# Both passes of a three-stage kernel by seven products for eight, with one class for the layers

## The chip, the cores and the metric

The kernel runs on one core of a Trainium2 chip. PE (TensorE) multiplies matrices, DVE (VectorE), ACT (ScalarE) and POOL (GpSimd) work element by element, and SP (SyncE) issues most of the transfers between the chip's memory and SBUF. The metric is device time in microseconds of one execution.

## What is computed

Four batches of twelve heads of sigmoid attention, 448 positions of 64 numbers each; then two layers on the 1792 tokens, each 768 to 2048 to 768:

```python
scores = scale * np.matmul(q, k.transpose(0, 1, 3, 2)) - np.log(S)
attn = 1.0 / (1.0 + np.exp(-scores))
x = np.matmul(attn, v)            # then to (B * S, H * D)
...
h = x @ w_in                      # first layer
x = (h - np.tanh(h)) @ w_out
...
h = x @ w_in                      # second layer
r = np.maximum(h, 0.0)
return (s * (r * r) + b) @ w_out
```

The layers' weights arrive as 64-bit floats and are turned into 32-bit ones on the chip.

## The kernel before

The tokens are taken in two passes of two batches, 896 tokens each. A pass is an attention over 12 pairs of heads and then the two layers. Line 82 of the profile is the helper that records every instruction in program order, so all rows carry that line and are told apart by the names of their tiles.

*Attention.* For pair `i`, `qk(i, c)` makes a chunk of scores (tile `sc`, then ACT's sigmoid into `af`), `prep(i + 1)` turns the next pair's q and k on PE by the identity (`tqk`) and splits them into high and low parts (`qt`, `kt`, and an unsplit copy `qkf`), and `av(i - 1)` multiplies by the values (`o`). An engine takes its instructions strictly in the order written. Between these steps stand loads, conversions and splits of the first weights, on DVE alone, since ACT is full of sigmoids.

*Precision.* Each product of the layers is three matmuls, high by high, high by low and low by high. A split is a copy on ACT (`whi`, `g`, `x`) and a subtraction on DVE (`wlo` and so on).

*Weights.* A chunk of 128 x 768 numbers is loaded as pairs of 32-bit words (`raw`), converted in four steps (`w_conv`: an ACT or DVE multiply into `wy`, a DVE shift of every second word into `wa`, two DVE steps with two sources into `wa` and `wf`), written to scratch memory and split. In the second pass chunks come from the scratch as `wf`. `w_in` is taken by four chunks to a group, `w_out` by four more, and four groups make a layer.

*First pass.* `layer1`, `layer2`: for each of four chunks of a group `hidden` makes 6 x 3 matmuls on 512 and on 384 tokens (tile `h`), 144 to a group. Then come the output products (`y` 144 matmuls to a group, `z` 168). The order of the work beside them is written by hand: `w_ahead` is called at fixed places and loads, converts or splits the next chunks.

*Second pass.* The class `Second` makes a pair of chunks by two token halves as a two-by-two block product with seven block products for eight (Winograd's form): sums and differences of the four weight blocks (`ws`) and of the four token blocks (`xo`, "t1" to "t4") are split, multiplied in PSUM banks `hs`, and added (`p`). A pair is 7 x 3 x 3 = 63 matmuls of 448 columns. A `Plan` collects all of its operations with an engine, a guessed cost and the keys that they read and write. Then `emit` goes through them as a list scheduler: PE and SP keep their written order, and ACT, DVE and POOL take from what is ready the one that is due first. What it emits is a fixed program; the costs are used for the order only.

*Seam of the passes.* The first scores of the second attention are made between the last `z` products. SBUF is split for good between the attention's tiles, the conversion's and the layers', with a few pools released for the second pass.

Of the kernel before, what the change touches and what calls it, by code (L numbers as in the profile page):

```python
# [19 lines left out]
def tile_kernel(ctx, tc, q, k, v, w_in1, w_out1, w_in2, w_out2, s_in, b_in, out):  # L20
# [16 lines left out]
    nc = tc.nc  # L37
# [26 lines left out]
    at_p = tc.alloc_tile_pool(name="at", bufs=1, side="right")  # L64
    conv_p = tc.alloc_tile_pool(name="conv", bufs=1)
    ps_p = tc.alloc_tile_pool(name="ps", bufs=1, space=PSUM)
    late = {}
# [18 lines left out]
    def banks(name):  # L86
        return ps_p.tile([P, 2, 512], F32, tag="two", name=name, bufs=3)

    turn = [0]

    def bank(name):

        turn[0] += 1
        return banks(name)[:, 0] if turn[0] % 5 % 2 == 0 else ps_p.tile([P, 512], F32, tag="one", name=name, bufs=2)
# [16 lines left out]
    scratch, raw_t, f_t, w_t = {}, {}, {}, {}  # L111

    def w_load(n, alone=False):
        if n >= len(chunks):
            return
        key = chunks[n]
        if key not in scratch:
            t = conv_p.tile([P, WE, 2], U32, tag="raw", name="raw", bufs=3)
            a = CC if key[0] == "in" else 2
            sp.dma_start(out=t.rearrange("p (a f) t -> p a f t", a=a), in_=w_src(key))  # L120
            raw_t[n] = t
        else:
            t = w_p.tile([P, WE], F32, tag="wf", name="wf", bufs=5)
            sp.dma_start(out=t, in_=scratch[key])
            f_t[n] = t

    def w_conv(n, alone=False):

        if n >= len(chunks) or n in f_t:
            return
        key = chunks[n]
        r = raw_t.pop(n)
        a = conv_p.tile([P, WE], U32, tag="wa", name="wa", bufs=2)
        y = conv_p.tile([P, WE], F32, tag="wy", name="wy", bufs=2)  # L140
        t = w_p.tile([P, WE], F32, tag="wf", name="wf", bufs=5)
        if alone:
            dve.tensor_scalar(y, r[:, :, 1].bitcast(F32), 2.0 ** -112, None, op0=ALU.mult)
        else:
            act.activation(y, r[:, :, 1].bitcast(F32), AF.Copy, scale=2.0 ** -112)
        yield
        dve.tensor_scalar(a, r[:, :, 0], 29, None, op0=ALU.logical_shift_right)
        yield
        dve.scalar_tensor_tensor(out=a, in0=y.bitcast(U32), scalar=3, in1=a, op0=ALU.logical_shift_left, op1=ALU.bitwise_or)
        dve.scalar_tensor_tensor(out=t.bitcast(U32), in0=y.bitcast(U32), scalar=0x80000000, in1=a, op0=ALU.bitwise_and, op1=ALU.bitwise_or)  # L150
        scratch[key] = dram.tile([P, WE], F32, name=f"w{key[0]}{key[1]}_{key[2]}_{key[3]}")
        sp.dma_start(out=scratch[key], in_=t)
        f_t[n] = t

    def w_split(n, alone=False):
        if n >= len(chunks):
            return
        t = f_t.pop(n)
        hi = w_p.tile([P, WE], F32R, tag="whi", name="whi", bufs=4)
        lo = w_p.tile([P, WE], F32R, tag="wlo", name="wlo", bufs=4)  # L160
        (dve.tensor_copy if alone else act.copy)(hi, t)
        yield
        dve.tensor_tensor(out=lo, in0=t, in1=hi.bitcast(F32), op=ALU.subtract)
        w_t[n] = (hi, lo)

    done = {w_load: 0, w_conv: 0, w_split: 0}

    def upto(step, n, **kw):

        while done[step] <= (n if step is w_load else min(n, len(a_pass) - 1)):  # L170
            yield from step(done[step], **kw) or ()
            done[step] += 1

    def w_ahead(n, parts="ab"):

        yield from upto(w_load, n + 5)
        for part in parts:
            if part == "a":
                yield from upto(w_conv, n + 3)
            else:  # L180
                yield from upto(w_split, n + 2)

    def now(g):
        for _ in g:
            pass

    def mm3(ps, w, ws, x, xs, first, last):

        pe.matmul(ps, w[0][:, ws], x[:, 0, xs], start=first, stop=False)
        pe.matmul(ps, w[0][:, ws], x[:, 1, xs], start=False, stop=False)  # L190
        pe.matmul(ps, w[1][:, ws], x[:, 0, xs], start=False, stop=last)

    def split(hi, lo, t):
        act.copy(hi, t)
        dve.tensor_tensor(out=lo, in0=t, in1=hi.bitcast(F32), op=ALU.subtract)


    raws, ready, avs, flt, x_t = {}, {}, {}, {}, {}

    def qkv_load(i, what="qkv"):  # L200
        if i >= B * NP:
            return
        b, hs = i // NP, slice(i % NP * 2, i % NP * 2 + 2)
        if "q" in what:
            raws[i] = {"r": at_p.tile([P, 2, D], F32, tag="rawr", name="rawr", bufs=3)}
# [21 lines left out]
    def prep(i):  # L227

        if i >= B * NP:
            return  # L230
        b = i // NP
        rq, rk, rr = (raws[i][nm] for nm in "qkr")
        both = banks("tqk") if i else None


        if i:
            flat = both.rearrange("p a b -> p (a b)")
            parts = [(flat, 0), (flat, SM + P), (flat, SM)]
        else:

            one = [ps_p.tile([P, 512], F32, tag="one", name="tqk0", bufs=2) for _ in range(2)]
            parts = [(one[0], 0), (one[1], P), (one[0], SM), (one[1], 0)]
        for (ps, o), r in zip(parts, (rk, rq) if b % 2 else (rq, rk)):
            for j in range(NJ):
                pe.transpose(ps[:, o + j * P:o + (j + 1) * P], r[:, j].rearrange("p h d -> p (h d)"), ident)
        for ps, o in parts[2:]:
            pe.transpose(ps[:, o:o + P], rr.rearrange("p h d -> p (h d)"), ident)
        tq, tk = (flat[:, 0:S], flat[:, S:2 * S]) if i else (one[0][:, 0:S], one[1][:, RM:P + SM])
        if b % 2:
            tq, tk = tk, tq  # L250
        qt = at_p.tile([P, 2, S], F32R, tag="qt", name="qt", bufs=2)
        kt = at_p.tile([P, 2, S], F32R, tag="kt", name="kt", bufs=2)
        act.copy(qt[:, 0], tq)
        act.copy(kt[:, 0], tk)
        for t, ps in ((qt, tq), (kt, tk)):
            dve.tensor_tensor(out=t[:, 1], in0=ps, in1=t[:, 0].bitcast(F32), op=ALU.subtract)

        flt[i] = tmp_p.tile([P, WN], F32, tag="t2", name="qkf", bufs=2)
        dve.tensor_copy(flt[i], (flat if i else one[0])[:, SM:S + S] if b % 2 else (flat if i else one[0])[:, 0:S + RM])
        ready[i] = qt, kt  # L260
        avs[i] = []

    def qk(i, c):
# [3 lines left out]
        sc = banks("sc")  # L267
# [20 lines left out]
    def av(i):  # L288

        b, hp = i // NP, i % NP  # L290
        rv, af = raws.pop(i)["v"], avs.pop(i)
        o = ps_p.tile([P, 512], F32, tag="one", name="o", bufs=2)[:, :S]

        o2 = ps_p.tile([P, 512], F32, tag="one", name="o2", bufs=2)[:, :SH]
        for c in range(NJ):
            for e in range(2):
                pe.matmul(o[e * D:e * D + D], rv[:, e, c, :], af[c // 2][:, c % 2, e], start=c == 0, stop=False)
        for h in range(2):
            for e in range(2):
                ks = slice(h * RM, h * RM + RM)  # L300
                pe.matmul((o2 if h else o[:, :SH])[e * D:e * D + D], rv[ks, e, NJ, :], af[1][ks, 1, e, :SH], start=h == 1, stop=True)
        yield
        half = tmp_p.tile([P, WN], F32, tag="t1", name="half", bufs=2)[:, :SH]
        act.copy(half, o2)
        dve.tensor_tensor(out=o[:, SH:], in0=o[:, SH:], in1=half, op=ALU.add)
        yield
        if b >= B // 2:
            yield from sums_of_x(b, hp, o)
            return
        if b % 2 == 0:  # L310
            x_t[b // 2, hp] = x_p.tile([P, 2, T2], F32R, tag="x", name="x1", bufs=CC)
        ns = slice(b % 2 * S, b % 2 * S + S)
        xt = x_t[b // 2, hp]
        split(xt[:, 0, ns], xt[:, 1, ns], o)


    def activate(layer, ps, hi, lo, fill):

        n = ps.shape[1]
        t = tmp_p.tile([P, WN], F32, tag="t1", name="t1", bufs=2)[:, :n]  # L320
        g = tmp_p.tile([P, WN], F32, tag="t2", name="t2", bufs=2)[:, :n]
        if layer == 0:
            act.activation(t, ps, AF.Tanh)
            dve.tensor_tensor(out=g, in0=ps, in1=t, op=ALU.subtract)
            next(fill, None)
        else:
# [4 lines left out]
        act.copy(hi, g)  # L331
        next(fill, None)
        dve.tensor_tensor(out=lo, in0=g, in1=hi.bitcast(F32), op=ALU.subtract)
        now(fill)

    pos = [0]

# [750 lines left out]
```

## Time and profile before

| what | us |
|---|---|
| median of 3 runs | 1089.71 (1089.34 to 1090.09) |
| the profiled execution | 1090.19 |
| its span, first to last instruction | 1088.4 |
| PE busy | 1073.2 (99%) |
| DVE busy | 698.7 (64%) |
| ACT busy | 536.5 (49%) |

The span is what the views cover, and the rest of the execution lies around it. Busy shares are means over stages that differ, so they say which engine to look at and not what an edit is worth. TensorE was granted its full clock throughout.

### The profile page before, as it was taken

To read this page: it belongs to the slowest core of one execution; us is meant where nothing else is said; L and a number is where in the kernel's file an instruction comes from. 1 tells how busy PE (TensorE), PEld (TensorE's weight loads), DVE (VectorE), ACT (ScalarE), POOL (GpSimd) and SP (SyncE) were. 2 spreads that over 40 slices of the span, in tenths; PEclk is the share of its full clock that TensorE was granted. 3 is DMA by queue.
4 is the path that set the end of the run, shared out by engine and by line. 5 is a ranking of instruction groups with operands and counts; after the bars stand their busy time and mean duration, and the time that the engine had idled before them with its cause. 6 is when DMAs were issued, how large, how long until landed. Compare 5 with 4: busy or idle time off the path is not lost.

```text
span 1088.4 us, 15221 instructions
## 1 busy us (share of the span) xinstructions
PE 1073.2 (99%) x5933; PEld 933.6 (86%) x5933; DVE 698.7 (64%) x1075; ACT 536.5 (49%) x867; POOL 61.5 (6%) x90
## 2 busy tenths in 40 slices
PE   7999999999999999999999999999999999999998
PEld 4557889888988999999985569999999999999998
DVE  2564656777787657676737778374757982747462
ACT  4775444241536654453527766351515584717170
POOL 4222000000000000000005400000000000000000
PEclk9999999999999999999999999999999999999999
DMA  7574464546445545454454403121112031212002
GB/s 188 153 194 137 131 202 146 174 136 212 131 132 173 191 157 175 144 179 156 140 164 114 105 2 117 44 66 51 58 52 65 15 102 44 73 42 75 30 1 102
DMA packets 104840, 124.47 MB, mean 114 GB/s; under 512 B 50080, under 2 KB 78240, under 8 KB 104768
## 3 DMA queue, kind: packets, MB, share of 16 engines
q1 hardware_dynamic: 100832, 116.94, 35.3%
q0 software_dynamic: 3136, 6.36, 2.1%
q8 instruction: 47, 0.77, 0.3%
q10 hardware_dynamic: 800, 0.20, 0.1%
q14 instruction: 25, 0.20, 0.1%
HBM read 92.80 MB, written 30.67 MB: 113 GB/s over the span
## 4 chain that ended last, share of the span: by engine, by line
PE 95%; DVE 2%; ACT 1%; POOL 1%; issue 0%; ACTq 0%; DVEq 0%; POOLq 0%
PE hs L82 41%; PE h L82 21%; PE z L82 11%; PE y L82 10%; PE o L82 6%; PE sc L82 5%; PE tqk L82 2%; POOL rawv L82 1%; ACT af L82 1%; DVE wa L82 0%; DVE qkf L82 0%; DVE x L82 0%; DVE kt L82 0%; DVE y L82 0%; DVE qt L82 0%
## 5 line engine op out<-in xcount | busy, mean ns | idle before, releaser
L82 PE MATMUL h<-x,whi 128*128 128x512 f32 (+1 forms) x768 | 217.3, 363 | 0.0
L82 PEld LDWEIGHTS h<-x,whi 128*128 128x128 f32 x768 | 141.7, 188 | 17.2 <-issue 0.6
L82 PE MATMUL hs<-xo,whi 128*128 128x448 f32 x504 | 153.4, 368 | 1.3 <-ACT af L82 1.2
L82 PE MATMUL hs<-xo,wlo 128*128 128x448 f32 x504 | 154.2, 368 | 0.0
L82 PE MATMUL h<-x,wlo 128*128 128x384 f32 (+1 forms) x384 | 139.9, 364 | 0.0
L82 ACT CAST whi<-wf 128x768 fp32r<-128x768 f32 x108 | 87.7, 812 | 66.8 <-DVE wf L82 57.1
L82 PE MATMUL hs<-whi,g 128*128 128x384 f32 x448 | 115.2, 335 | 0.0
L82 PE MATMUL z<-whi,g 128*128 128x384 f32 x448 | 115.1, 335 | 0.0
L82 DVE TENSOR_TENSOR wlo<-wf,whi 128x768 fp32r<-128x768 f32 x104 | 99.9, 961 | 19.9 <-ACT whi L82 13.5
L82 DVE TENSOR_TENSOR g<-t,g 128x448 fp32r<-128x448 f32 (+2 forms) x128 | 79.2, 622 | 50.0 <-ACT g L82 49.9
L82 PE MATMUL hs<-g,whi 128*128 128x448 f32 x384 | 110.1, 368 | 0.0
L82 ACT ACTIVATE af<-sc,nlogs 128x896 f32<-128x896 f32 (+1 forms) x96 | 86.2, 927 | 47.6 <-PE sc L82 37.1
L82 PE MATMUL y<-g,whi 128*128 128x384 f32 (+1 forms) x384 | 109.4, 366 | 0.2 <-DVE y L82 0.2
L82 PEld LDWEIGHTS hs<-xo,whi 128*128 128x128 f32 x504 | 94.7, 188 | 11.3 <-ACT af L82 1.5
L82 PEld LDWEIGHTS hs<-xo,wlo 128*128 128x128 f32 x504 | 94.7, 188 | 9.2 <-ACT p L82 0.5
L82 ACT CAST g<-t 128x448 fp32r<-128x448 f32 (+2 forms) x128 | 72.1, 567 | 28.5 <-DVE t L82 26.4
L82 DVE TENSOR_TENSOR y<-hs,y 128x384 f32<-128x384 f32 (+1 forms) x79 | 46.1, 588 | 60.0 <-PE hs L82 59.9
L82 PEld LDWEIGHTS z<-whi,g 128*128 128x128 f32 x448 | 81.0, 188 | 0.6 <-issue 0.6
L82 PEld LDWEIGHTS hs<-whi,g 128*128 128x128 f32 x448 | 81.1, 188 | 0.2
L82 PEld LDWEIGHTS y<-g,whi 128*128 128x128 f32 x384 | 71.2, 188 | 9.1 <-DVE y L82 0.6
L82 PEld LDWEIGHTS h<-x,wlo 128*128 128x128 f32 x384 | 72.0, 188 | 7.6
L82 PEld LDWEIGHTS hs<-g,whi 128*128 128x128 f32 x384 | 72.1, 188 | 7.0
(100 smaller groups left out, 1624.9 us busy)
## 6 DMA issues: line engine op xcount, KB each, us to landing
raw<-in_moe_w_in_dram SPq DMA_DIRECT2D x32, 768.0 KB, 5.2
raw<-in_moe_w_out_dram SPq DMA_DIRECT2D x32, 768.0 KB, 4.7
win<-wf SPq DMA_DIRECT2D x32, 384.0 KB, 2.6
wout<-wf SPq DMA_DIRECT2D x32, 384.0 KB, 2.7
wf<-win SPq DMA_DIRECT2D x32, 384.0 KB, 3.0
wf<-wout SPq DMA_DIRECT2D x32, 384.0 KB, 3.0
rawq<-in_q_dram SPq DMA_DIRECT2D x48, 96.0 KB, 3.5
rawv<-in_v_dram POOLq DMA_DIRECT2D x24, 192.0 KB, 3.6
```

The source lines that it names most:

```text
L82: return lambda *a, **kw: tc.keep_in_program_order(getattr(self.engine, name)(*a, **kw))
```

## The change

- `Second` becomes `Layers(sb)`, used in both passes, and `layer1`, `layer2`, `hidden`, `w_ahead` and the conversion by hand go. So the first pass, too, has seven products for eight and a list that is scheduled, now with conversions in the list. SP is scheduled by due time as well, and a cost can have a busy and a done part.
- A conversion works in place in `raw` (words two apart) and writes `wf`; `wa` and `wy` go. The weight sums are made in place in two `wf` tiles.
- Slots for split weights (`w`), `wf`, `raw` and `p` are taken and given back as their last use is written: 12 `w` slots in the first pass, 18 in the second, where there were 4 + 4 and 14.
- The relu of a stored sum is one DVE step on the sum alone, without ACT's part.
- The identity is built before the value loads are issued.
- The attention's tiles and the layers' share SBUF in turn (`open_pool`, `close_pool`). `prep` of pair 12 is made two tiles ahead of the end of the first pass, and its scores follow in the second attention. Pairs 12 and 13 are loaded in the last output products (`next_loads`), and pair 14 after them.

```diff
-    def w_conv(n, alone=False):
...
-        a = conv_p.tile([P, WE], U32, tag="wa", name="wa", bufs=2)
-        y = conv_p.tile([P, WE], F32, tag="wy", name="wy", bufs=2)
...
-        dve.tensor_scalar(a, r[:, :, 0], 29, None, op0=ALU.logical_shift_right)
...
+        def conv(self, n):
...
+            r, t = self.raw[rk], f_t[k]
+            y, a = r[:, :, 1], r[:, :, 0]
...
+                self.do("ACT", 0.74, lambda: act.activation(y.bitcast(F32), y.bitcast(F32), AF.Copy, scale=2.0 ** -112), w=[("r", rk)])
+            self.do("DVE", 0.47, lambda: dve.tensor_scalar(a, a, 29, None, op0=ALU.logical_shift_right), w=[("r", rk)])
+            self.do("DVE", 0.88, lambda: dve.scalar_tensor_tensor(out=a, in0=y, scalar=3, in1=a, op0=ALU.logical_shift_left, op1=ALU.bitwise_or), w=[("r", rk)])
+            self.do("DVE", 0.88, lambda: dve.scalar_tensor_tensor(out=t.bitcast(U32), in0=y, scalar=0x80000000, in1=a, op0=ALU.bitwise_and, op1=ALU.bitwise_or), r=[("r", rk)], w=[("f", k)])
...
+        def w_pair(self, n):
...
+            self.conv(n)
+            self.conv(n + 1)
...
+            kh, kl = self.w_whole(k0)
...
+            sums = ((v1[:, 1], v1[:, 0], v1[:, 1], ALU.add, k1), (v1[:, 0], v0[:, 0], v1[:, 0], ALU.subtract, k1), (v0[:, 0], v1[:, 1], v0[:, 0], ALU.subtract, k0), (v0[:, 1], v0[:, 1], v0[:, 0], ALU.subtract, k0))
+            for o, a, b, op, k in sums:
+                self.do("DVE", 0.47, lambda o=o, a=a, b=b, op=op: dve.tensor_tensor(out=o, in0=a, in1=b, op=op), r=[("f", k0), ("f", k1)], w=[("f", k)])
...
+            if final and not self.sb:
+                self.next_loads()
+            for t in range(last):
+                if final and not self.sb and t == last - 2:
+                    self.next_prep()
...
+    qkv_load(0, "qk")
+    make_identity(nc, ident)
+    for i, what in ((1, "qk"), (0, "v"), (1, "v"), (2, "qkv")):
...
-    make_identity(nc, ident)
-    prep(0)
+    prep(0, [one("tqk0"), one("tqk0")])
...
+        layers = Layers(sb)
+        layers.early = layers.w_pair(layers.n0)
+        loads = {2: 2, 4: 1, 6: 1, 8: 1, 10: 1}
+        convs = {5: 1, 6: 1, 8: 1, 10: 1}
...
+        layers.run(i1 - 1)
```

POOL at the start of the program, before: the last of nine value loads (`rawv`), which stand behind two loads of `rawr` (the last rows of q and k of pair 0), and then the identity:

```order
L82 DMA rawv<-in_v_dram 64x2x64 x2
L82 DMA rawv<-in_v_dram 128x2x192
L82 DMA rawv<-in_v_dram 64x2x64
masks.py:197 MEMSET ident 128x128
masks.py:199 ISA
masks.py:199 AFFINE_SELECT ident<-ident 128x128
```

and POOL at the same place after the change:

```order
L86 DMA rawr<-in_k_dram 64x2x64
masks.py:197 MEMSET ident 128x128
masks.py:199 ISA
masks.py:199 AFFINE_SELECT ident<-ident 128x128
L86 DMA rawv<-in_v_dram 64x2x64
L86 DMA rawv<-in_v_dram 128x2x192
```

The identity moved ahead of all nine value loads, behind the two loads of `rawr`.

DVE in the first layer of the first pass, in the products by `w_in`, before (`t`, `g`: activation):

```order
L82 TENSOR_SCALAR wa<-raw 128x768
L82 TENSOR_TENSOR g<-t_2626,g 128x512
L82 SCALAR_TENSOR_TENSOR wa<-wy,wa 128x768
L82 SCALAR_TENSOR_TENSOR wf<-wy,wa 128x768
L82 TENSOR_TENSOR t_2662<-h,t_2661 128x384
L82 TENSOR_TENSOR wlo<-wf,whi 128x768
L82 TENSOR_TENSOR g<-t_2662,g 128x384
```

and DVE in the same stretch after the change:

```order
L86 TENSOR_TENSOR wf<-wf 128x3x128 x4
L86 TENSOR_TENSOR y<-hs,y 128x448 x2
L86 TENSOR_SCALAR raw<-raw 128x768
L86 TENSOR_TENSOR w<-wf,w 128x768
L86 SCALAR_TENSOR_TENSOR raw<-raw 128x768
L86 TENSOR_TENSOR p<-hs,p 128x448
L86 TENSOR_TENSOR w<-wf,w 128x768
L86 SCALAR_TENSOR_TENSOR wf<-raw 128x768
L86 TENSOR_TENSOR t<-p,t 128x448
```

The conversion's three steps are now taken apart by other work, and the weight sums (`wf<-wf`) and the sums of kept products (`p<-hs,p`) are new.

PE in the first layer of the first pass, before, a piece of one chunk (numbered `x` tiles are the six input blocks):

```order
L82 MATMUL h<-x_625,whi 128x512 x2
L82 MATMUL h<-x_625,wlo 128x512
L82 MATMUL h<-x_708,whi 128x512 x2
L82 MATMUL h<-x_708,wlo 128x512
L82 MATMUL h<-x_294,whi 128x384 x2
L82 MATMUL h<-x_294,wlo 128x384
```

and PE after the change, from the first group's end on:

```order
L86 MATMUL hs<-g,w 128x448 x132
L86 MATMUL hs<-xo,w 128x448 x108
L86 MATMUL hs<-g,w 128x448 x12
L86 MATMUL hs<-xo,w 128x448 x18
L86 MATMUL hs<-g,w 128x448 x132
```

A group of the first layer has 126 hidden matmuls of 448 columns (108 and 18) where it had 144 of 512 or 384, and the same 144 output matmuls.

## Rows read from the trace of the kernel before

**Rows 1.** The page: engine, busy us (share of the span), instructions

```profile
PE 1073.2 (99%) x5933; PEld 933.6 (86%) x5933; DVE 698.7 (64%) x1075; ACT 536.5 (49%) x867; POOL 61.5 (6%) x90
```

**Rows 2.** Chain of work that ended last: start us, us, what

```profile
89.49 2.94 PE h L82 x12
...
151.28 29.07 PE h L82 x144
...
549.90 0.76 PE tqk L82 x7
...
554.86 0.80 PE sc L82 x5
...
563.11 0.78 PE tqk L82 x7
...
638.40 231.80 PE hs L82 x1130
...
1085.10 0.56 DVE y L82
```

**Rows 3.** Busy us by stage; its columns are in the first line

```profile
core 0: us, PE busy (x) PEld busy (x) DVE busy (x) ACT busy (x) POOL busy (x), PEclk, DMA share, GB/s
...
8.96:89.49 80.53, 77.63 (x618) 44.72 (x618) 42.28 (x72) 57.07 (x92) 21.88 (x35) 1.00 0.69 175
89.49:327.20 237.71, 237.55 (x1173) 209.89 (x1174) 164.35 (x235) 96.81 (x154) 3.01 (x5) 1.00 0.50 157
327.20:563.90 236.70, 236.68 (x1279) 223.07 (x1281) 161.48 (x236) 116.69 (x178) 0.00 (x0) 1.00 0.51 165
...
638.40:871.50 233.10, 233.03 (x1136) 210.33 (x1136) 156.42 (x254) 105.00 (x181) 0.00 (x0) 1.00 0.18 55
871.50:1085.10 213.60, 213.49 (x1140) 204.40 (x1140) 122.20 (x197) 103.11 (x172) 0.00 (x0) 1.00 0.19 59
```

**Rows 4.** PE: longest waits, in us in total, times, longest

```profile
PE tqk L82 <- POOL ident masks.py:199: 4.2, 1, 4.2
```

**Rows 5.** Timeline at the start: start us, us, engine, instruction

```profile
0.74 2.91 SPq L82 DMA_DIRECT2D rawq<-in_q_dram  x4
...
1.99 0.60 POOL L82 DMA_DIRECT2D rawr<-in_k_dram  x1
```

**Rows 6.** DMA issues of the first 20 us: count, KB each, median us to landing

```profile
rawq<-in_q_dram SPq DMA_DIRECT2D x10, 96.0 KB, 3.5
...
rawr<-in_k_dram POOLq DMA_DIRECT2D x1, 32.0 KB, 3.6
```

**Rows 7.** DVE groups by shape: busy us, mean ns of one, idle before

```profile
L82 DVE TENSOR_TENSOR wlo<-wf,whi 128x768 fp32r<-128x768 f32 x104 | 99.9, 961 | 19.9 <-ACT whi L82 13.5 <-PE hs L82 5.2
...
L82 DVE SCALAR_TENSOR_TENSOR wa<-wy,wa 128x768 uint32<-128x768 uint32 x64 | 61.2, 956 | 9.0 <-ACT wy L82 5.2
...
L82 DVE TENSOR_SCALAR wa<-raw 128x768 uint32<-128x768 uint32 x64 | 35.3, 552 | 0.0
L82 DVE TENSOR_TENSOR p<-hs,p 128x448 f32<-128x448 f32 x50 | 30.9, 620 | 17.8 <-PE hs L82 15.1 <-ACT p L82 2.1
...
L82 DVE TENSOR_TENSOR ws<-wf 128x384 f32<-128x384 f32 x32 | 18.6, 583 | 5.5 <-DMA wf<-win 5.4
...
L82 DVE CAST whi<-wf 128x768 fp32r<-128x768 f32 x3 | 1.7, 551 | 0.0
```

**Rows 8.** DVE timeline around one conversion in the first attention

```profile
46.94 0.96 DVE L82 SCALAR_TENSOR_TENSOR wa<-wy,wa 128x768 uint32<-128x768 uint32 x1
47.93 0.96 DVE L82 SCALAR_TENSOR_TENSOR wf<-wy,wa 128x768 uint32<-128x768 uint32 x1
48.81 0.62 DVE L82 TENSOR_TENSOR qt<-tqk,qt 128x448 fp32r<-128x448 f32 x1
49.34 0.61 DVE L82 TENSOR_TENSOR kt<-tqk,kt 128x448 fp32r<-128x448 f32 x1
```

**Rows 9.** PE timeline, two microseconds later

```profile
50.70 1.49 PE L82 MATMUL sc<-qt,kt 64*128 64x448 f32 x12 [0.62 <-ACT half L82]
```

More of the change, by code (lines that the diff above doesn't have):

```diff
@@ L97, in tile_kernel, with __init__, take, give @@
+    class Slots:
+        def __init__(self, n):
+            self.free = list(range(n))
+        def take(self):
+            return self.free.pop(0)
+        def give(self, k):
+            assert k not in self.free
+            self.free.append(k)
     words = [w.bitcast(U32).rearrange("r (c t) -> r c t", t=2) for w in (w_in1, w_out1, w_in2, w_out2)]
@@ L174, in w_ahead @@
[L174 to L198, printed above, removed]
+    scratch = {}
+    W_EARLY, W_LATE, W_MORE, F_SLOTS, R_SLOTS, P_SLOTS = 5, 7, 6, 4, 3, 6
+    w_t = [w_p.tile([P, WE], F32R, tag=f"w{k}", name="w") for k in range(W_EARLY)]
+    f_t = [w_p.tile([P, WE], F32, tag=f"f{k}", name="wf") for k in range(F_SLOTS)]
+    raws, ready, avs, flt = {}, {}, {}, {}
     def qkv_load(i, what="qkv"):
@@ L306, in av @@
         yield
[L307 to L326, printed above, removed]
-            act.activation(t, ps, AF.Relu)
-            dve.scalar_tensor_tensor(out=t, in0=ps, scalar=0.0, in1=t, op0=ALU.max, op1=ALU.mult)
-            next(fill, None)
-            act.activation(g, t, AF.Identity, bias=b_sb, scale=s_sb)
[L331 to L334, printed above, removed]
@@ L845, in group @@
-            a0, c0, vs0 = a, c, vs
+            if first:
+                self.first_pair(n, i)
+            else:
+                now(self.w_pair(n))
+                left = self.pair_open(layer, n, 0, range(NJ - 1) if grp == 0 else None)
+            now(self.w_pair(n + 2))
             m = n + 2
-            a, b = self.bank(), self.bank()
+            a, b = self.b.take(), self.b.take()
             self.prod(a, m, "11", "11", start=True)
@@ new lines, in next_prep @@
+        def next_prep(self):
+            b0, b1 = self.b.take(), self.b.take()
+            self.keys = {"tq": ("b", b0), "tk": ("b", b1)}
+            as_key = lambda ks: [self.keys.get(k, k) for k in ks]
+            prep(2 * NP, [self.whole[b0], self.whole[b1]], lambda eng, cost, fn, r=(), w=(): self.do(eng, cost, fn, as_key(r), as_key(w)))
+            self.b.give(b0)
+            self.b.give(b1)
+    raw_pool = open_pool("raw_w")
+    at = open_pool("qk", side="right")
+    open_pool("raw_qkv", side="right")
```

959 lines of the change are left out of this document (422 added, 537 removed).

## The prediction, made before the changed kernel ran

> **What bounds the kernel now.** I read the page's busy shares first, to see which engine can set the time at all, then the chain that ended last, to see where its links run, then the stages. PE is busy 1073.2 us of a span of 1088.4, DVE 698.7 [rows 1]. The chain shows why that is more than an average: in both passes it is one matmul after another, in pieces of tens or hundreds of us, so a matmul taken out of the stream shortens the time, and anything added on another engine costs nothing until PE has to wait for it [rows 2]. The stages show the room that is left: in the first pass DVE works 164.35 of 237.71 us and then 161.48 of 236.70, ACT 96.81 and 116.69; in the second pass DVE has 156.42 of 233.10 and 122.20 of 213.60 [rows 3]. PE idles for hardly 0.2 us in each of these. Outside them one wait of PE stands out: 4.2 us at the start, for the identity that POOL makes [rows 4].
>
> **The products.** The first pass runs from 89.49 to the end of the transpose at 563.11 + 0.78 = 563.89, which is 474.40 us. In it stand matmuls of the second attention that PE must do in either kernel: 0.76, two of 0.80 (the two score chunks), 0.78, together 3.14 [rows 2]. So the first pass itself is 471.26. Its last pair of heads' value products lie inside, as they do in the second pass. The second pass, which already makes seven products of eight and has 448 columns in each of its first-layer matmuls, runs from 638.40 to 1085.10, or 446.70, with PE never idle [rows 2, 3]. The changed first pass issues the same products in the same shapes, instruction for instruction, so I take the second pass's length for it: **-24.6 us**. A cross-check from the other side: 144 hidden products take 29.07 us now [rows 2]; an eighth of the eight such groups is 29.1. The second pass keeps less than that, since its narrower matmuls take 231.80/1130 = 0.2051 us each against 29.07/144 = 0.2019 for 512 and 384 columns together. I use the smaller gain, since it is measured whole.
>
> **The start.** POOL now builds the identity behind two small loads instead of behind nine more of the values. Then data ends PE's wait. SP's four rawq issues take 2.91 us from 0.74, so the second one starts near 1.5, and a load lands 3.5 us after its issue: about 5.0, or 5.7 if that counts from the issue's end. POOL's last rawr issue is at 1.99 for 0.60, and lands 3.6 later, at 5.6 to 6.2, for the last two of eight transposes [rows 5, 6]. PE's wait ended at 8.96; I take 5.3: **-3.7 us**, between -2.8 and -4.2 (the whole wait [rows 4]). The value loads start later by the identity's few instructions; their first reader stands in the second iteration.
>
> **DVE in the first pass.** Here the change pays. Each pair of input chunks now needs four sums of 384 elements and difference splits of 768, 768, 768 and 384, where it needed two splits of 768; and each pair of hidden chunks needs three additions of kept products. The order counts 379 DVE instructions between the first product of the pass and the last product of the second layer's first pair, the stretch with the densest DVE work (it holds the preparation of the second layer's input): 113 with two sources and 768 elements, 35 shifts, 184 of 448, 45 of 384, 2 small ones of about 0.4. With 0.958, 0.552, 0.620 and 0.583 us each they sum to 108.3 + 19.3 + 114.1 + 26.2 + 0.8 = 268.7 us [rows 7]. That is the upper bound, each instruction behind the end of the last. The lower: qt starts 0.88 us after wf, which lasts 0.96, and kt 0.53 after qt's start, which lasts 0.62; where an instruction is ready it starts some 0.08 before the one ahead ends. wf itself, which reads what wa wrote, started 0.99 after wa of 0.96 [rows 8]. With 0.08 off all 379 the sum is 238.4. PE needs 1185 matmuls there, ten of which the trace counts double, 1195 x 0.2051 = 245.1 us. So PE waits between 0 and 23.6 us. The in-place steps of a conversion read each other's output, while the list puts other work between many of them, so I take the middle, 253.5: **+8 us**, spread over the first layer and the start of the second. Over the rest of the pass DVE has slack: in the whole pass some 634 instructions sum to 453 us, less 51, middle 427, against 446.7. ACT stays far below: 391 instructions for 327, at the present mean of (96.81 + 116.69)/332 = 0.64 us, are some 250 us [rows 3].
>
> The Trainium skill, VectorE: DVE Perf Modes, section The DRAIN you can't avoid, says the opposite of the 0.08: the next Vector instruction does not start until the pipe is empty. By that the upper sum would hold and the wait be 23.6; the trace disagrees wherever the next instruction is ready [rows 8].
>
> In-place conversion removes the wa and wy buffers and no instruction; I cost it at nothing, since a shift reading every second word takes 0.552 us and a cast of contiguous words 0.551 [rows 7]. That no row shows a strided write is the slower rival below.
>
> **Attention and seams.** In the first attention 100 DVE instructions stand for 75, among them a fourth conversion (0.55 + 0.55 + 0.96 + 0.96 = 3.0 us) and the sums of x. One conversion ahead of qt and kt left PE a gap of 0.62 us [rows 9]. In iterations 8 to 10 DVE has two conversions, two odd pairs' sums (seven instructions, some 4.1) and one set of weight sums (2.9): about 25 us with prep's share, 22 after overlap, against three iterations of 80.53/12 = 6.7 [rows 3]. That is 2 to 5 over, of which the next iteration, without prep, takes some back: +2.5. The loads of pair 14 now stand on SP behind the 14 stores of the first pass; pairs 12 and 13 are loaded before them. Their landing of 3.5 us is hidden by pair 12 and 13's scores up to a small rest: +0.5. Together **+3 us**, between 0 and +8. What hides the other new work (POOL's sums, SP's waits for slots, the shared SBUF) is PE's own stream of 446.7; uncovered, each would show as a PE wait in the same place.
>
> **Sum**, on the profiled execution's 1090.19 (span 1088.4 and 1.8 around it): 1090.19 - 24.6 - 3.7 + 8 + 3 = 1072.9. The median of the runs shown is 1089.71, 0.48 lower, so I forecast **1072.4 us**.
>
> **Rivals.** *DVE hidden throughout.* The list starts DVE's work early enough, as it does in the second pass, where PE never waits for it [rows 3]; against it, 238.4 of 245.1 us is a full engine. Then 1090.19 - 24.6 - 3.7 - 0.48 = 1061.4.
>
> *DVE becomes the bound of the first layer.* Each in-order wait on ACT or on the scratch write of a chunk, which the in-place sums must let finish, eats the 0.08. For it speaks that 379 instructions leave no idle time; against it, that DVE ran 164 us in this layer's stage without making PE wait [rows 3]. Price: 23.6 instead of 8, and 6 for attention: 1091.0, no gain at all.
>
> *Slower: words two apart.* After the change, the 120 two-source steps of 60 conversions in the pass read both sources at every second word, half of them write so too. If an operand at that step costs a second element time, each takes longer by twice 0.956 - 0.552 = 0.81 us [rows 7], 97 us in all; DVE then needs 427 + 97 = 524, PE follows it, and the time is 1090.19 + 524 - 471.3 - 3.7 + 3 - 0.5 = about 1142. It decides from 0.37 us an instruction on, where DVE needs 472. Against it stands the shift's 0.552, which is a read only.
>
> The Trainium skill, Vector Engine (DVE) Microarchitecture Reference, section Measured stream behaviour on trn2, has the rule for it: a port runs at full rate only over runs of two adjacent words or more. By its rule the shift ought to be slow too, and the trace disagrees for the read; for a write no run here shows it.
>
> **How the numbers follow.** The likeliest case, with waits of DVE between 3 and 15 us, gives 1066 to 1080 and has 0.55. DVE hidden has 0.19, DVE as the bound 0.15 (1084 to 1093, about half of it faster), words two apart 0.08, a load or a slot that holds up the pass 0.03. A difference under 0.2% (2.2 us) is what a measurement here can't tell from none: faster 0.82, the same 0.06, slower 0.12. The range 1062 to 1088 leaves out the strided case, the upper half of the bound case and a sliver below.
>
> **What would show it.** Right: the first pass's chain in PE pieces of hs, its length 446 to 462 us; PE's first transpose at 5 to 6 us; DVE busy about 420 us in the pass; PE waits there for DVE, most of them around the second layer's first products. Wrong: two-source steps of raw longer than 0.96 us; PE waiting all along the second layer as well; a wait for rawq at the seam; a gap of PE after the last score of the first attention of several us.

## The result and the profile after

The changed kernel takes 1080.57 us (median of 4 runs, 1079.39 to 1081.91) beside 1089.69 for the kernel before on the same chip: a ratio of 0.9917, with a 95% interval of 0.9899 to 0.9934. It is faster by 9.1 us, where 17.3 were forecast; the time lies inside the range, though just outside the 1066 to 1080 that the prediction gave its likeliest case. The profiled execution took 1081.91, its span 1080.1. The page, which answers to [rows 1]:

```profile
PE 1055.4 (98%) x5790; PEld 920.7 (85%) x5790; DVE 793.5 (73%) x1264; ACT 562.8 (52%) x912; POOL 73.2 (7%) x100
```

PE is busy for 17.8 us less and DVE for 94.8 more. The stages, with the columns of [rows 3]: start, first attention, first pass in two parts, second attention, second pass in two parts, end.

```profile
0.00:5.63 5.63, 3.36 (x4) 1.20 (x5) 0.44 (x2) 1.49 (x2) 4.50 (x13) 1.00 0.56 128
5.63:91.66 86.03, 78.91 (x618) 44.48 (x618) 57.83 (x94) 58.46 (x94) 33.34 (x43) 1.00 0.68 176
91.66:318.00 226.34, 223.22 (x1085) 202.00 (x1086) 214.39 (x333) 129.06 (x207) 0.00 (x0) 0.99 0.53 168
318.00:545.31 227.31, 225.93 (x1203) 215.25 (x1201) 195.69 (x306) 119.23 (x187) 7.66 (x12) 1.00 0.50 156
545.31:626.58 81.27, 76.60 (x610) 42.99 (x609) 45.10 (x78) 58.06 (x93) 27.71 (x34) 0.96 0.41 105
626.58:861.00 234.42, 232.91 (x1135) 210.25 (x1136) 159.97 (x262) 108.58 (x185) 0.00 (x0) 1.00 0.20 61
861.00:1076.80 215.80, 214.51 (x1143) 204.49 (x1141) 119.48 (x192) 87.89 (x147) 0.00 (x0) 1.00 0.18 56
```

The differences, stage by stage, before and after. The first pass ends exactly at 545.24, with the first score of pair 12; 0.79 us of transposes for that pair lie inside it and are counted with the second attention, as in the forecast.

| stage | before | after | difference | forecast |
|---|---|---|---|---|
| start | 8.96 | 5.63 | -3.33 | -3.7 |
| first attention | 80.53 | 86.03 | +5.50 | +2.5 |
| first pass | 471.26 | 452.79 | -18.47 | -16.6 |
| second attention | 77.65 | 82.13 | +4.48 | +0.5 |
| second pass | 446.70 | 450.22 | +3.52 | 0 |
| sum | | | -8.30 | -17.3 |

The chain of work, which answers to [rows 2], runs through DVE at the first pass's opening and again around the second layer's start, from 267 to 346 us; for the rest of the pass it is PE:

```profile
96.42 0.97 DVE raw L86
...
112.83 1.08 ACT t L86 x2
115.03 148.51 PE hs L86 x716
267.36 1.06 DVE y L86 x2
...
346.48 198.83 PE hs L86 x1070
```

From 267.36 to 346.48 DVE is busy 78.53 of 79.12 us, so it has no slack left there, but PE waits only 1.29 us of that.

So the products' gain came, and a little more; the two attentions and the second pass gave 13.5 us back. Where PE waited, in us in total, times, longest:

```profile
PE hs L86 <- ACT p L86: 6.6, 7, 2.7
PE sc L86 <- DVE qt L86: 5.4, 2, 2.8
...
PE tqk L86 <- DMA rawq<-in_q_dram: 0.9, 1, 0.9
...
PE hs L86 <- DVE w L86: 0.4, 1, 0.4
```

Three of these waits by PE's timeline, in the first attention, at the first pass's opening and at the second layer's start:

```profile
78.63 1.61 PE L86 MATMUL sc<-qt,kt 64*128 64x448 f32 x10 [2.51 <-DVE qt L86]
...
115.03 5.17 PE L86 MATMUL hs<-xo,w 128*128 128x448 f32 x17 [2.69 <-ACT p L86]
...
330.12 10.14 PE L86 MATMUL hs<-xo,w 128*128 128x448 f32 x48 [1.03 <-ACT p L86]
```

The 4.2 us for the identity [rows 4] are gone and 0.9 for data have come. The DVE groups of a conversion, which answer to [rows 7]:

```profile
L86 DVE SCALAR_TENSOR_TENSOR raw<-raw 128x768 uint32<-128x768 uint32 x64 | 61.2, 956 | 5.0 <-ACT raw L86 2.3 <-DVE raw L86 0.5
L86 DVE SCALAR_TENSOR_TENSOR wf<-raw 128x768 uint32<-128x768 uint32 x64 | 60.8, 954 | 0.9
...
L86 DVE TENSOR_SCALAR raw<-raw 128x768 uint32<-128x768 uint32 x64 | 37.3, 583 | 0.0
```

Reading and writing every second word costs the two-source steps nothing (956 ns before). The shift's mean rose from 552 to 583, and that is not the stride either. In the first attention POOL's sum of x and a shift, by POOL's and DVE's timelines:

```profile
42.56 1.38 POOL L86 TENSOR_TENSOR y<-xo 128x448 f32<-128x448 f32 x1 [1.16 <-DVE xo L86]
```

```profile
42.86 1.50 DVE L86 TENSOR_SCALAR raw<-raw 128x768 uint32<-128x768 uint32 x1
```

The shift starts 0.30 us after POOL and ends 0.42 after it: it lasts 1.50 instead of 0.55, as if it had stood still until POOL was through. The Trainium skill, SBUF — State Buffer, section Who interferes with whom, has this as a rule: DVE and GpSimd share a port pair, a tensor_scalar can be one of the DVE forms that take it, and the engine that comes second is blocked for the whole of the other's instruction. The trace agrees.

In the second attention, DVE around the step with the half split and the four sums, then PE, then the granted clock (in the column before the last two):

```profile
599.27 0.62 DVE L86 TENSOR_TENSOR qt<-tqk,qt 128x448 fp32r<-128x448 f32 x1 [2.03 <-ACT kt L86]
...
606.39 0.62 DVE L86 TENSOR_TENSOR xo<-y,xo 128x448 fp32r<-128x448 f32 x1
606.93 0.54 DVE L86 CAST w<-wf 128x384 fp32r<-128x384 f32 x1
607.51 0.56 DVE L86 TENSOR_TENSOR w<-wf,w 128x384 fp32r<-128x384 f32 x1
608.11 2.34 DVE L86 TENSOR_TENSOR wf<-wf 128x384 f32<-128x384 f32 x4
610.36 0.62 DVE L86 TENSOR_TENSOR qt<-tqk,qt 128x448 fp32r<-128x448 f32 x1
```

```profile
611.04 2.39 PE L86 MATMUL sc<-qt,kt 64*128 64x448 f32 x10 [2.85 <-DVE qt L86]
613.36 0.90 PE L86 MATMUL tqk<-ident,rawk 128*128 128x128 f32 x3
```

```profile
607.00:609.00 2.00, 1.18 (x8) 0.50 (x8) 1.90 (x5) 1.78 (x3) 0.00 (x0) 1.00 0.00 0
609.00:611.00 2.00, 0.00 (x0) 0.00 (x0) 1.93 (x5) 0.00 (x0) 0.00 (x0) 0.69 0.00 0
611.00:613.00 2.00, 1.96 (x10) 1.46 (x10) 1.97 (x4) 0.00 (x0) 0.00 (x0) 0.50 0.00 0
613.00:615.00 2.00, 2.00 (x11) 1.35 (x7) 0.70 (x2) 1.89 (x3) 0.00 (x0) 0.50 0.00 0
```

Behind an even pair of heads, which has two sums and splits of x, DVE is idle for 2.03 us ahead of qt. Behind this odd one, which has seven, they end at 606.93, 3.4 us of weight steps follow, and only then comes qt. PE stands for 2.85 us, and its clock falls to half (1.2 GHz) and stays there for some 6 us: three transposes take 0.90 us, where they take 0.55 at the full clock. PE's busy time in this attention, from its first score, is 76.67 us, and 73.92 in the run after_even below, where the stall is gone and the products are the same: so the stall costs some 2.7 us beyond its length, by the clock.

### The profile page after: what moved, and what is told of

It is laid out like the page before. It is cut to its first block, busy times and chain, and to the rows that moved or that the text cites. A ratio compares the mean times of both kernels' runs of the same rounds, so it can differ in the third digit from the quotient of the medians.

```text
span 1080.1 us, 15112 instructions
## 1 busy us (share of the span) xinstructions
PE 1055.4 (98%) x5790; PEld 920.7 (85%) x5790; DVE 793.5 (73%) x1264; ACT 562.8 (52%) x912; POOL 73.2 (7%) x100
## 4 chain that ended last, share of the span: by engine, by line
PE 80%; DVE 15%; ACT 3%; issue 2%; DMA 0%; DVEq 0%; SPq 0%; ACTq 0%
PE hs L86 70%; PE o L86 5%; PE sc L86 4%; DVE wf L86 3%; DVE xo L86 2%; DVE w L86 2%; PE tqk L86 2%; DVE p L86 2%; DVE raw L86 2%; DVE y L86 1%; DVE t L86 1%; DVE g L86 1%; ACT af L86 0%; ACT w L86 0%; ACT t L86 0%
## 5 line engine op out<-in xcount | busy, mean ns | idle before, releaser
L86 PE MATMUL hs<-xo,w 128*128 128x448 f32 x2016 | 423.7, 369 | 8.4 <-ACT p L86 6.6
L86 PEld LDWEIGHTS hs<-xo,w 128*128 128x128 f32 x2016 | 378.4, 189 | 48.7 <-ACT p L86 10.8
L86 PE MATMUL hs<-g,w 128*128 128x448 f32 x1152 | 239.0, 367 | 0.0
L86 ACT CAST w<-wf 128x768 fp32r<-128x768 f32 (+1 forms) x186 | 145.0, 784 | 180.0 <-PE hs L86 118.4
L86 PE MATMUL hs<-w,g 128*128 128x384 f32 x1344 | 236.9, 336 | 0.0
L86 PEld LDWEIGHTS hs<-w,g 128*128 128x128 f32 x1344 | 234.4, 188 | 0.6
L86 PEld LDWEIGHTS hs<-g,w 128*128 128x128 f32 x1152 | 216.4, 188 | 20.0
L86 DVE TENSOR_TENSOR w<-wf,w 128x768 fp32r<-128x768 f32 (+1 forms) x192 | 170.5, 894 | 67.8 <-ACT w L86 59.1
L86 DVE TENSOR_TENSOR g<-t,g 128x448 fp32r<-128x448 f32 x128 | 77.4, 618 | 16.4 <-ACT g L86 16.4
L86 ACT CAST g<-t 128x448 fp32r<-128x448 f32 x128 | 71.7, 566 | 27.8 <-DVE t L86 26.0
```

The source lines that it names most:

```text
L86: return lambda *a, **kw: tc.keep_in_program_order(getattr(self.engine, name)(*a, **kw))
```

## The experiments

Times are medians; the kernel before stood at 1090.0 to 1090.2 beside them, and ratios are against it. Unless it says otherwise, a run is the changed kernel (1080.57, ratio 0.9917) with the edit shown. The first pass is counted with its 0.79 us of transposes here: 453.58 for the changed kernel, and 81.34 for its second attention.

**behind_prep and earlier** ask whether the place of the weight steps on DVE costs the attentions their time.

```diff
+            if i + 1 < i1:
+                prep(i + 1)
             for _ in range(convs.get(i - i0, 0)):
...
             if i - i0 in (7, 9, 11):
                 next(layers.early, None)
-            if i + 1 < i1:
-                prep(i + 1)
```

> Only the place of the early weight work in the attention loop changes: conversions and splits of the first weights now stand on DVE behind the next pair's qt, kt and qkf, not ahead of them. Theory A (order): PE's gaps in the attentions (sc waiting for DVE qt or qkf: 2.5 and 2.9 us the two longest) come from weight work standing in front, and the half clock after the gap in the second attention from the gap. Then attention 1 goes from 86.0 to 82 to 83 us and attention 2 from 82.1 to 77.5 to 79, in all 5 to 8 us less than the changed kernel. Rival B (amount): DVE simply has too much to do in iterations 8 to 11; the gap moves to the value products, whose bank comes free later, and the total changes by -1 to +2 us.

Measured: 1087.82, ratio 0.9977 (0.9968 to 0.9987), 7 us slower. The first attention took 92.84, the second 81.84. Theory A in this form fell: the order that was to help hurts, and worse than rival B said. PE in the first attention:

```profile
81.02 1.79 PE L86 MATMUL sc<-qt,kt 64*128 64x448 f32 x12 [2.32 <-DVE qkf L86]
...
96.58 0.41 PE L86 MATMUL o<-af,rawv 64*64 64x224 f32 x2 [2.40 <-DVE xo L86]
```

Behind prep the weight steps hold up the value products' bank (`xo` reads it), and the x steps then run into the next prep. The waits named qkf are for PSUM in all likelihood: `sc` and `tqk` share three tiles, and qkf is the last reader of one.

For `earlier`:

```diff
-        loads = {2: 2, 4: 1, 6: 1, 8: 1, 10: 1}
-        convs = {5: 1, 6: 1, 8: 1, 10: 1}
+        loads = {1: 2, 3: 1, 4: 1, 5: 1, 6: 1}
+        convs = {3: 1, 4: 1, 5: 1, 6: 1}
...
-            if i - i0 in (7, 9, 11):
+            if i - i0 in (7, 8, 9, 11):
```

and a `yield` between the second and the third of the four sums.

> Same work and same place ahead of prep, but spread: conversions in iterations 3, 4, 5, 6 for 5, 6, 8, 10, loads earlier to match, and the step with the half split and four sums cut in two (iterations 8 and 9). Theory A (order) and rival B (amount) both give attention 1 some 3 to 4 us back, since two conversions leave the full iterations 8 and 10. In attention 2, which converts nothing, they differ: A gives 3 to 4.5 us back, because no burst ahead of qt is longer than 2.2 us and the clock stays up; B gives under 1.5, because iterations 8 to 11 hold the same work.

Measured: 1078.89, ratio 0.9895 (0.9883 to 0.9908). The second attention fell by 3.0, at the lower edge of A, outside B; but a gap of 2.13 us is left there, and the clock fell behind it, which A had ruled out. The first rose to 88.15, against both: each conversion that is moved to an early iteration brings a gap of its own (1.56, 0.54, 0.82, 0.89 us).

**true_costs** gives the list the durations that the trace shows, in 25 of its lines with a cost on ACT or DVE.

```diff
-            self.do("DVE", 0.54, lambda: dve.tensor_tensor(out=self.pt[o], ...
+            self.do("DVE", 0.62, lambda: dve.tensor_tensor(out=self.pt[o], ...
```

> The costs that the list scheduler is given are set to the durations of the trace (DVE 0.54 to 0.62, 0.88 to 0.96, 0.47 to 0.55 to 0.58; ACT 0.43 to 0.53, 0.74 to 0.84 or 0.92, and so on); nothing else. Theory C: PE's waits in the two passes (hs for ACT p, 6.6 us in 7 waits; hs for DVE, about 1.7) come from a list that believes DVE and ACT some 12% faster than they are and starts weight work too late. Then the first pass goes from 452.9 to 447 to 450 us and the second from 450.2 to 447 to 448.5: 4 to 8 us less. Rival D: the waits come from the first pair of each pass, where everything is due at once and no order helps; then the change is within 1.5 us.

Measured: 1085.16, ratio 0.9957 (0.9945 to 0.9969). C is right for the second pass, 447.94 for 450.22, and wrong for the first, 459.64 for 453.58; D fits neither pass. In the first pass new waits stand at the second layer's start, on PE:

```profile
325.35 1.11 PE L86 MATMUL hs<-xo,w 128*128 128x448 f32 x2 [1.26 <-DVE xo L86]
...
331.24 2.61 PE L86 MATMUL hs<-xo,w 128*128 128x448 f32 x6 [1.50 <-DVE xo L86]
```

The costs of before were not guessed too low: behind a step of 0.62 the next one, if ready, starts 0.53 later, as kt behind qt in [rows 8], so 0.54 is what it costs an engine that is never idle. Here DVE is just that, from 317 to 343 us. In the second pass it is far from it, which may be why the longer costs help there; that was not tried by itself.

**identity_late** undoes the move of the identity.

```diff
-    make_identity(nc, ident)
     for i, what in ((1, "qk"), (0, "v"), (1, "v"), (2, "qkv")):
         qkv_load(i, what)
+    make_identity(nc, ident)
```

> One edit undone: the identity is built behind the nine value loads again. If the start's gain is the identity's and nothing else's, the first transpose is back near 8.96 us from 5.63 and the time is 3.3 us longer than the changed kernel (3 to 3.6). Rival: the first scores wait for something else soon after (loads of pair 1, DVE's zeroing), and part of the 3.3 is taken back: 1 to 2 us.

Measured: 1085.82, 5.2 us longer, ratio 0.9956 (0.9944 to 0.9968). That is longer than either expectation. In the traces, the first transpose came at 8.97, which is the 3.3. The first attention took 87.99, 1.96 longer with the same gaps: here the clock fell to half after its gap of 2.52 us, which it did not do in the changed kernel's own trace. The first pass took 452.10, 1.48 shorter: there the changed kernel's clock fell and this one's did not. So the identity is worth 3.3. The clock makes two traces differ by as much as the rest, but that it makes the difference between the medians is not shown.

**sums_on_act** takes POOL's sum of x away from the conversions.

```diff
-            pool.tensor_tensor(out=f, in0=xo[nm][j][:, 0].bitcast(F32), in1=xo[nm][j][:, 1].bitcast(F32), op=ALU.add)
+            act.copy(f, o)
```

> The copy of x that the attention keeps (y) is made by ACT from the PSUM bank, not by POOL as a sum of the two halves; POOL keeps only the four subtractions of y. In the changed kernel's trace the shift of a conversion takes 1.47 us, not 0.55, when POOL's sum (1.38 us) runs beside it, and ends 0.43 after it. Theory E (DVE waits while POOL reads): in attention 1 both slow shifts go back to 0.55 to 0.6, the PE gaps at iterations 5 and 6 (1.53 and 0.55) fall to about 0.6 and 0, and attention 1 is 1.3 to 2.5 us shorter; attention 2, which converts nothing, keeps its gap of 2.9. Rival F: ACT, full of sigmoids, passes its six further copies of 0.53 us a pass on to the scores, and the time grows by 1 to 3 us.

Measured: 1085.31, ratio 0.9961 (0.9948 to 0.9973). Theory E holds for its mechanism: the shifts of the first attention are back at 0.55,

```profile
L86 DVE TENSOR_SCALAR raw<-raw 128x768 uint32<-128x768 uint32 x4 | 2.2, 555 | 0.0
```

and the gap of 1.53 us at iteration 5 is gone. That at iteration 6 is not: it is 0.80 for 0.55. Rival F holds for the time: ACT's copy waits 0.69 us for DVE and then lasts 0.53, and PE waits 0.7 to 1.1 in every second iteration instead (attentions 87.02 and 83.97, where E had the first shorter by 1.3 to 2.5).

**after_even** moves the early steps of the second attention from behind odd pairs to behind even ones.

```diff
-            if i - i0 in (7, 9, 11):
+            if i - i0 in ((6, 8, 10) if sb else (7, 9, 11)):
```

> In the second attention only, the three early steps on the first weights move from iterations 7, 9, 11 to 6, 8, 10, that is from behind the long sums of an odd pair of heads to behind the short ones of an even pair; same work, nothing split. Theory A (order, as the run that spread the work left it): PE's gap of 2.85 us before qt falls below 1 us and the half clock after it goes, so attention 2 is 3.5 to 4.5 us shorter than 81.3 and the total 3.5 to 4.5 less than the changed kernel. Rival B (amount): a gap of 2 us or more appears at iteration 8 or 10 instead, and the total is within 1 us.

Measured: 1075.94, ratio 0.9874 (0.9861 to 0.9888), 4.6 us less than the changed kernel. The second attention took 76.79 for 81.34, at a clock of 1.00 throughout, with these gaps left on PE:

```profile
601.33 1.49 PE L86 MATMUL sc<-qt,kt 64*128 64x448 f32 x12 [1.55 <-DVE qkf L86]
...
608.63 1.50 PE L86 MATMUL sc<-qt,kt 64*128 64x448 f32 x12 [0.78 <-DVE qkf L86]
```

That is theory A's saving, just above its range, though the gap that is left is 1.55 and not below 1. Of the 4.55, 2.75 are PE's busy time, which is the clock, and 1.8 its waits. The work is the same, so B is out for this attention, and the loss there was the place of these steps.

**second_shift and no_sign_step** load and unload DVE in the first pass.

```diff
+            if not alone:
+                self.do("DVE", 0.47, lambda: dve.tensor_scalar(a, a, 0, None, op0=ALU.logical_shift_right), w=[("r", rk)])
```

> Each of the 60 conversions of the first pass that stand in the list gets one more DVE step, a shift by nothing (0.55 us each, 0.47 from start to start, 28 us in all, 15 of them before the second layer's first pair). Theory G (DVE is nearly full there and any step costs): the first pass is 10 to 28 us longer than 453.6. Rival H (DVE has slack, and the pass's 6 us of loss come only from the first pairs of the two layers): 0 to 5 us longer.

Measured: 1090.14, ratio 1.0001 (0.9992 to 1.0010); the first pass took 461.77, 8.2 more, between G and H.

```diff
-            self.do("DVE", 0.88, lambda: dve.scalar_tensor_tensor(out=t.bitcast(U32), in0=y, scalar=0x80000000, in1=a, op0=ALU.bitwise_and, op1=ALU.bitwise_or), r=[("r", rk)], w=[("f", k)])
```

(with the step ahead of it writing `t`; the steps of the attention keep theirs)

> The last step of the 60 listed conversions (which puts the sign back; the weights of the first pass lose their signs) is left out: 60 x 0.96 us of DVE less, 0.88 from start to start, 53 us in all. Theory G (DVE's load costs the first pass its 6 us over the second): the pass falls to 447 to 449 us, with PE's waits for ACT p and DVE w there gone. Rival H (the waits come from the order at the pass's opening, before most conversions): they stay, and the pass is within 1.5 us of 453.6.

Measured: 1076.41, ratio 0.9874 (0.9860 to 0.9887); the first pass took 447.98, in G's range, though 1.10 and 0.38 us of the waits for ACT p are left, of 4.42 in all. Without its 0.79 of transposes that is 447.2, the 446.7 of the second pass of before within 0.5. So DVE's load is what the first pass loses by, 5.6 us of it, but softly: 28 us more cost 8.2. The list plans anew in both runs, so that they change the order along with the load; what order alone gives is in late_start below.

**first_too** is after_even with the first attention changed alike.

```diff
-            if i - i0 in ((6, 8, 10) if sb else (7, 9, 11)):
+            if i - i0 in ((6, 8, 10) if sb else (7, 11)):
```

> The run after_even, and in the first attention too the step with the half split and the four sums leaves iteration 9: it goes to 11, where no later pair is prepared, and the split that stood there is left to the pass's list. Theory A (order): the gap of 2.51 us before qt in attention 1 goes, and with it the half clock that followed it in most traces (some 2 us); attention 1 falls from 86.0 to 82 to 83.5, while the pass takes the split, 1.4 us of DVE, for under 1 us: in all 2 to 4 us less than 1075.9. Rival B (amount): iteration 10, with a conversion, now shows the gap, or the pass's opening waits longer for its second weights; the total is within 1 us of 1075.9.

Measured: 1077.31, ratio 0.9882 (0.9868 to 0.9897). Theory A is out, and rival B's mechanism holds, though the total is 1.4 above and not within 1: against after_even the first attention fell by 1.7 to 84.33, and the first pass rose by 3.1 to 455.23, with 1.80 us for DVE w at its opening where there were 0.22, and the clock at half behind the next wait there (2.69), which it was not behind the same wait in after_even (2.72). A gap of 0.77 is left at iteration 9.

**pieces** cuts the first attention's steps to at most 1.8 us ahead of qt (`conv` made a generator with a `yield` after each DVE step), and lets DVE make the copy of x there.

```diff
-        convs = {5: 1, 6: 1, 8: 1, 10: 1}
+        loads = {2: 2, 4: 1, 6: 1, 8: 1, 10: 1} if sb else {1: 2, 3: 1, 6: 1, 8: 1, 9: 1}
+        convs = {3: (0, 0), 4: (0, 1), 5: (0, 1), 6: (1, 2), 7: (1, 2), 8: (2, 2)}
...
-            if i - i0 in ((6, 8, 10) if sb else (7, 9, 11)):
+            if i - i0 in ((6, 8, 10) if sb else (10, 11)):
...
+                dve.tensor_copy(f, o)
```

> In the first attention, the DVE steps on the first weights are cut so that at most 1.8 us stand ahead of qt, never behind an odd pair's long sums: three conversions (not four) in pieces over iterations 3 to 8, the first split at 10, the half split and sums at 11. The kept copy of x is made by DVE from PSUM there, not by POOL. The second attention as in the run after_even. Theory A with E (DVE's two idle microseconds ahead of qt are free, and a POOL sum beside it takes one of them): no PE gap above 0.8 us in attention 1, which falls to 79.5 to 82 us; the pass's opening, with a conversion and a split more, loses 1 to 2: 1071 to 1074 in all. Rival B (amount): the work only moves to the pass's opening, whose waits of 3 us double, and the total is 1075 or more.

Measured: 1074.27, ratio 0.9856 (0.9839 to 0.9872). The first attention fell to 81.21, as theory A with E had it, though with a gap of 1.03 (0.8 was its limit). The first pass took 454.02, 1.9 more than in after_even, and the total is 0.3 above theory A's range and 0.7 below B's. What B said of the pass's opening is seen there, in one wait of 4.39 us where there were 0.44 and 2.69; DVE, ACT and PE there:

```profile
92.17 0.96 DVE L86 TENSOR_TENSOR w<-wf,w 128x768 fp32r<-128x768 f32 x1
93.04 0.56 DVE L86 TENSOR_SCALAR raw<-raw 128x768 uint32<-128x768 uint32 x1
...
97.22 0.96 DVE L86 SCALAR_TENSOR_TENSOR wf<-raw 128x768 uint32<-128x768 uint32 x1
98.10 0.39 DVE L86 TENSOR_TENSOR hs<-hs,half 128x224 f32<-128x224 f32 x1
```

```profile
99.19 0.53 ACT L86 CAST xo<-hs 128x448 fp32r<-128x448 f32 x1 [4.36 <-DVE y L86]
...
100.35 0.54 ACT L86 COPY p<-hs 128x448 f32<-128x448 f32 x1
```

```profile
100.94 3.63 PE L86 MATMUL hs<-xo,w 128*128 128x448 f32 x10 [4.39 <-ACT p L86]
```

The list put a split and two conversions, 5.9 us, ahead of the sum of the last values. It takes DVE as free when the pass begins (87.05); DVE comes from the attention's last x steps at 92.05. ACT's `p` copy stands behind a cast that waits for that sum, and PE behind `p`.

**late_start** is pieces with DVE's and ACT's true start told to the list, and the costs of true_costs for the second pass alone.

```diff
-            free = dict.fromkeys(waiting, 0.0)
+            free = {**dict.fromkeys(waiting, 0.0), **late}
...
-            self.plan.emit()
+            self.plan.emit({} if self.sb else {"DVE": 5.0, "ACT": 4.4})
```

> On top of the run pieces, two edits of the list only, one for each pass, read apart by stage. First pass: the list is told that DVE is free 5.0 us and ACT 4.4 us after the pass begins (as that run's trace has it), where it took all engines as free at once; the order then has the last values' sum ahead of two conversions on DVE. Second pass: costs as long as the durations of the trace, as in the run true_costs, where this pass took 447.9. Theory I (PE's wait of 4.39 us at the pass's opening is that wrong start): the wait falls under 1.5 us and the first pass from 454.0 to 449 to 451.5; with 448 for the second, 1067.5 to 1070.5 in all. Rival J (DVE has too much to do at the opening, whatever the order): the wait moves to the next pair's weights, the first pass stays within 1 us of 454.0, and the total is 1071.5 to 1073.

Measured: 1066.45, ratio 0.9781 (0.9767 to 0.9794). DVE and the stages (first attention, first pass, second attention, second pass):

```profile
92.66 0.39 DVE L86 TENSOR_TENSOR hs<-hs,half 128x224 f32<-128x224 f32 x1
92.96 0.55 DVE L86 TENSOR_SCALAR raw<-raw 128x768 uint32<-128x768 uint32 x1
```

```profile
5.43:86.67 81.24, 77.44 (x617) 44.63 (x618) 53.70 (x92) 59.35 (x95) 25.99 (x37) 1.00 0.65 172
86.67:538.01 451.34, 447.91 (x2285) 415.76 (x2286) 412.16 (x644) 248.43 (x394) 7.68 (x12) 1.00 0.53 165
538.01:614.62 76.61, 73.72 (x610) 41.82 (x609) 45.18 (x78) 56.96 (x92) 27.75 (x34) 1.00 0.46 117
614.62:1062.30 447.68, 446.48 (x2278) 414.99 (x2276) 281.31 (x454) 197.24 (x333) 0.00 (x0) 1.00 0.19 58
```

Theory I: PE's wait of 4.39 at the opening is gone, with one of 1.43 us at 108 us and one of 1.31 late in the pass; the first pass took 451.34, 2.7 less, and the second the expected 448; the total is 1 us below its range. This version takes 14.1 us less than the changed kernel and 23.6 less than the one before: the first attention gave 4.8, the first pass 2.2, the second attention 4.7, the second pass 2.5.

## Why the prediction was right and wrong

*The products, right.* -24.6 was the second pass's length put for the first's. With DVE unloaded the first pass comes to 447.2, which is -24.1.

*DVE in the first pass, near in size, wrong in place.* The +8 measured +6.1 (452.79 less 446.70), and no_sign_step shows that 5.6 of it go with DVE's load. It was to lie around the second layer's first products; there it was 1.29 us (1.03 and 0.26). Most lay at the opening: 0.44 for DVE w and 2.69 for ACT p, and behind the latter the clock was at half for some 3 us (PE's busy time in the pass is 449.07, and 447.81 in after_even's trace, where it did not fall: 1.3). DVE was busy 410 us of the forecast 420, and around the second layer's start, where the text had it full, it was (78.53 of 79.12 us). But PE waited only 1.29 us there and more at the opening, so that 6.1 lies near 8 is in part luck.

One reading in that term needs setting right. The prediction says that the Trainium skill, VectorE: DVE Perf Modes, section The DRAIN you can't avoid, is against the 0.08. The same section adds that a next op which is not held starts earlier, so starts 0.88 and 0.53 us apart [rows 8] do not contradict it.

*The start, right.* -3.33 for -3.7, with PE waiting for data as said; the loads landed 0.3 later than taken.

*Attention and seams: here the prediction failed.* Its step "+3 us, between 0 and +8" measured +9.98. For the first attention it added up DVE's work over three iterations and let the next take the surplus back: +2.5, measured +5.50, of which pieces gives 4.8 back. What counts is the place: two microseconds ahead of qt are free behind an even pair and none behind an odd one (after_even, pieces), and PE's gap shows as soon as they are exceeded. It also counted POOL's sums among the work that PE's stream hides; in the first attention two shifts beside them took 0.95 us longer each, on the path to qt. For the second attention it priced only the loads of pair 14, at +0.5, and these cost nothing that shows: no PE wait there names a load. The weight steps, at new places there too, were left out: measured +4.48, of which after_even gives 4.55 back.

*The second pass: a term that was missing.* The text took its length for both passes and did not cost the second one's own new order. It lost 3.52: 2.6 in four waits for ACT's `p` copies, the rest in PE's busy time (447.42 for 446.52 in [rows 3]). Longer costs in the list take 2.3 to 2.5 back (true_costs, late_start), so it is the order; which of the moved steps does it was not tried. That the time stayed in the range all the same is the range's width: two terms priced at +3 and 0 measured +9.98 and +3.52.

*The rivals.* DVE hidden throughout is out by 6.1 us. DVE as the bound, at 23.6, is out by 17.5 the other way: the chain does run through DVE for 79 us, but PE waited 1.29 us there and not at all between 346 us and the pass's end. Words two apart is out by [rows 7] beside the rows above, 956 and 954 ns.

*Where the gain went.* Of 17.3 us, 8.3 came, 9.0 did not: 7.0 in the attentions and 3.5 in the second pass, plus 0.4 at the start, less 1.9 that the first pass did better. The run late_start changes only orders, the costs and starts that the list goes by, and the engine that makes one copy, and it gets 14.1 back.

## What to carry to other kernels

Price a burst on an in-order engine by the slack at its own place (what is due right behind it, and what was just ahead), not by the work of a few iterations. A list scheduler's plan is as good as its first state: tell it when each engine really comes free, and give it costs from start to start for an engine that is full. When the bound falls in one stage, cost the other stages' new orders as well, since a few stalls of 0.4 to 3 us, and the slower clock behind some of them, took back 13.5 of a gain of 25.

## What the hardware showed that was not expected

TensorE's granted clock fell to half (1.2 GHz) behind some of PE's stalls and stayed there for 3 to 7 us (10 in true_costs, behind several), and the same stall did it in one execution and not in the next. Seven traces have the 2.5 us at iteration 9 of the first attention, and it fell in five of them; behind the 2.7 to 2.9 us of the second attention it fell in six of six. In second_shift it fell behind waits of 1.31, 1.40 and 0.87 us close together, and in true_costs behind those from 321 to 331 us. In late_start, whose longest wait after the start is 1.57, it did not fall after the start. So a stall can cost twice its length. The runs of one kernel lie up to 2.5 us apart (1079.39 to 1081.91); that this is the reason is not shown, since one execution of each was traced.

At the start the column of the granted clock does not tell PE's speed. In five of the twelve traces since the change it shows half from 8 to 12 us, where PE waits twice for about 1 us; in the other seven, and in that of the kernel before, it shows 1.00. Yet in just those eight the first three transposes take 0.87 to 0.90 us, as at half the clock, and in the five 0.52; late_start and after_even:

```profile
5.43 0.87 PE L86 MATMUL tqk<-ident,rawq 128*128 128x128 f32 x3 [0.69 <-DMA rawq<-in_q_dram]
```

```profile
5.62 0.52 PE L86 MATMUL tqk<-ident,rawq 128*128 128x128 f32 x3 [0.91 <-DMA rawq<-in_q_dram]
```

So that TensorE had its full clock throughout in the kernel before holds for the column only. The changed kernel's trace is 0.9 us behind after_even's at 14 us, after the same instructions.

Two sources and a target at every second word cost a DVE step nothing (956 against 956 ns). The Trainium skill, Vector Engine (DVE) Microarchitecture Reference, section Measured stream behaviour on trn2, asks for runs of two adjacent words for a port's full rate; for these steps the trace disagrees, in the write too.
